# Last two head groups share one score unit: joining two half-filled units and keeping the emptied slot

## The chip, the cores and the metric

The kernel runs on one core of a Trainium2 chip. The metric is the device time of one execution in microseconds. Three runs of the kernel before gave 320.46, 319.23 and 320.46 us; the median is 320.46 us. One further execution was recorded by the hardware profiler, and all intervals below come from it.

## The reference

The input is a sequence of 2048 tokens with 640 features in bfloat16. It passes a layer norm and then two branches, whose product is added to the input:

```
xn = layernorm(x)
s  = attention(xn, wq, wk, wv, wo, beta)      # 32 heads of 20, in 4 segments of 512 tokens
g  = silu( (sigmoid(xn @ w_gate) * (xn @ w_up)) @ w_down )   # 640 -> 1536 -> 640
out = x + s * g
```

In the attention branch every segment of 512 tokens attends causally to itself only (softmax of q k / sqrt(20)). What earlier segments held comes in through a memory matrix per head, which is updated after each segment. A gate per head, sigmoid(beta), mixes the two.

## The kernel before, in words

**Segments and slots.** The four segments are worked through one after the other. The scores of a segment are cut by *head group* (4 heads, one per quarter of TensorE's rows; 8 groups, numbered 0 to 7) and by *key block* (128 keys; 4 blocks per segment, 0 to 3). Because the mask is causal, key block kb is met by the last 512 - 128 kb queries only. One entry `(g, kb, c0, ncol, q0)` says: group g, key block kb, put into columns c0 to c0 + ncol of the score tile, for the queries from q0 on. A *unit* is a list of such entries that together fill up to 512 columns of the score tile `Sps` (128 x 4 x 512 in PSUM, one buffer). A unit costs one *slot*.

**How units are formed.** `pair_units(g)` packs two head groups into five units: block 0 of g; blocks 1 and 3 of g; blocks 2 of g and of g + 1 together (256 + 256 columns); block 0 of g + 1; blocks 1 and 3 of g + 1. The last pair of the last segment, groups 6 and 7, is different: `single_units` gives each of them three units of its own, and block 2 stands alone in a unit of 256 columns. So there are 15 pairs of five units and one of six, 81 slots (numbers 0 to 80). Slots 75, 76, 77 are group 6; slots 78, 79, 80 are group 7; slots 77 and 80 are the half-filled ones.

**What a slot does.** `scores` (L548) writes the unit's scores into `Sps` with matmuls that use a quarter of TensorE's rows each. `exps` makes one ScalarE exponential over the unit (L556) into a tile `pt` (four buffers), and one GpSimd select per entry (L558), which zeroes the keys behind the mask. Then the slot is filled with *dense* work: `do_gate`, `do_up` and `do_down` matmuls (lines 130 and 134), which come from a queue `dense` and are handed out one matmul at a time. At the end of the last segment, these are the `yp` matmuls of `do_down`: 12 of them per tile, then a tanh on ScalarE (`t`, L454) and a multiply on VectorE (`aa`, L455).

**What orders the work.** The program is written out engine by engine. Events carry a time in slots (table `TIMES`), and a running account of matmul time (`due` against `done`, `rate` per slot) decides how many dense matmuls lie between two events. The account spreads all remaining work evenly over `SLOTS` slots.

**How probabilities meet values.** For all groups but 6 and 7 of the last segment, `attend_T` takes a whole group at once. Groups 6 and 7 of the last segment (slots from `OLD` = 75) use `attend` (L612): with time 1.36 slots after a unit's slot began, it multiplies that unit's `pt` with the values into `Aps`, one PSUM tile for the whole group with a place for each of the four query blocks. A matmul there has 21 output columns, and there are 4 heads times (4 - kb) query blocks for an entry. For group 7, `attend` calls `finalize` twice: after its third block of keys for query blocks 0 and 1, after its fourth for 2 and 3. For group 6 it calls it once. `finalize` is four VectorE instructions: reciprocal of the sums (L631), times the gate (L632), times `Aps` (L636, tile `od`), and an addition into `odot` (L638). L631 and L636 read `Aps`.

**The tail.** Two `do_down` items are held back. After the last slot: the first held item, `tail_T4` (two transposes of `odot` into `po`, L523, copied to `oT` on ScalarE, L524), then the `attend` of the last unit (slot 80), then for each of four token tiles two `tail_piece` (five matmuls with the output weights, L532, then a VectorE multiply, L534) and `tail_add` with the store, with the second held item and a second `tail_T4` between them.

Of the kernel before, what the change touches and what calls it, by code (L numbers as in the profile page):

```python
# [14 lines left out]
NSEG = 4  # L15
# [4 lines left out]
NG = 8  # L20
# [23 lines left out]
def pair_units(g):  # L44
    return [[(g, 0, 0, 512, 0)],
            [(g, 1, 0, 384, 128), (g, 3, 384, 128, 384)],
            [(g, 2, 0, 256, 256), (g + 1, 2, 256, 256, 256)],
            [(g + 1, 0, 0, 512, 0)],
            [(g + 1, 1, 0, 384, 128), (g + 1, 3, 384, 128, 384)]]

def single_units(g):
    return [[(g, 0, 0, 512, 0)],
            [(g, 1, 0, 384, 128), (g, 3, 384, 128, 384)],
            [(g, 2, 0, 256, 256)]]

def segment_units(n):
    units = []
    for g in range(0, NG, 2):
        last = n == NSEG - 1 and g == NG - 2
        units += single_units(g) + single_units(g + 1) if last else pair_units(g)  # L60
    return units

TIMES = dict(
# [18 lines left out]
def kernel(  # L82
# [437 lines left out]
    def tail_T4(j0, j1):  # L520
        po = ps_d.tile([P, 2, P], BF, name="po", tag="d")
        for j in range(j0, j1):
            nc.tensor.transpose(po[:, j - j0, :], seg[NSEG - 1]["odot"][:, j, C4:D], ident[:])  # L523
        nc.scalar.copy(seg[NSEG - 1]["oT"][:, DC - 1, j0 * P:j1 * P].rearrange("p (j t) -> p j t", t=P), po[:])  # L524

    def tail_piece(j, half):

        s, hs = seg[NSEG - 1], slice(half * HD, (half + 1) * HD)
        sp = ps_d.tile([P, HD], F32, name="sp", tag="d")
        for c in range(DC):  # L530
            oT = s["oTm" if c == 3 else "oT"]
            nc.tensor.matmul(sp[:], lhsT=oT[:, c, j * P:(j + 1) * P], rhs=Wo[:, c, hs],  # L532
                             start=(c == 0), stop=(c == DC - 1), skip_group_check=True)
        nc.vector.tensor_tensor(s["aa"][j][:, hs], s["aa"][j][:, hs], sp[:], op=ALU.mult)  # L534
# [10 lines left out]
    def scores(unit):  # L545
        for r in range(4):
            for (g, kb, c0, ncol, q0) in unit:
                nc.tensor.matmul(Sps[:, r, c0:c0 + ncol],  # L548
                                 lhsT=KT[32 * r:32 * r + DH + 3, g, kb * P:(kb + 1) * P],
                                 rhs=QT[32 * r:32 * r + DH + 3, g, q0:L],  # L550
                                 start=True, stop=True, tile_position=(32 * r, 0))

    def exps(unit):
        ntot = sum(u[3] for u in unit)
        pt = ptp.tile([P, 4, L], BF, name="pt")
        nc.scalar.activation(pt[:, :, 0:ntot], Sps[:, :, 0:ntot], ACT.Exp, scale=SCALE)  # L556
        for (g, kb, c0, ncol, q0) in unit:
            nc.gpsimd.affine_select(out=pt[:, :, c0:c0 + P], in_=pt[:, :, c0:c0 + P], compare_op=ALU.is_ge,  # L558
                                    fill=0.0, base=0, pattern=[[0, 4], [1, P]], channel_multiplier=-1)
        return pt  # L560

    def attend_T(n, g, todo):


        s = seg[n]
        if g % 4 == 0:
            s["obT", g // 4] = opool.tile([P, 4, L], BF, name="obT", bufs=1)
        ps = ps_d.tile([P, L], F32, name="ApsT", tag="d")
        for i, ((_, kb, c0, ncol, q0), t) in enumerate(todo):
            for r in range(4):  # L570
                off = (kb * H + 4 * g + r) * E1
                nc.tensor.matmul(ps[32 * r:32 * r + 32, q0:L], lhsT=Vflat[n % 2][:, off:off + 32],  # L572
                                 rhs=t[:, r, c0:c0 + ncol], start=(i == 0), stop=(i == len(todo) - 1),
                                 tile_position=(0, 32 * r), skip_group_check=True)
        tb = opool.tile([P, L // 32, 32], F32, name="tb", tag="tb", bufs=1)
        rb = opool.tile([P, L // 32], F32, name="rb", bufs=2)
        ob = obs[g % 2]

        def quotients():
            nc.vector.reciprocal(rb[:], tb[:, :, DH])  # L580
            if g == NG - 1:
                nc.vector.scalar_tensor_tensor(out=ob[:, :, 0:DH], in0=tb[:, :, 0:DH], scalar=omgT[:, g:g + 1],
                                               in1=rb[:].unsqueeze(2).to_broadcast([P, L // 32, DH]),
                                               op0=ALU.mult, op1=ALU.mult)
                return
            nc.gpsimd.tensor_scalar(rb[:], rb[:], omgT[:, g:g + 1], None, op0=ALU.mult)
            nc.gpsimd.tensor_tensor(ob[:, :, 0:DH], tb[:, :, 0:DH],  # L587
                                    rb[:].unsqueeze(2).to_broadcast([P, L // 32, DH]), op=ALU.mult)

        def turn_back():  # L590
            nc.vector.transpose(s["obT", g // 4][:, g % 4, :], ob[:].rearrange("p b e -> p (b e)"))  # L591

        s["turn", g] = (lambda: nc.vector.transpose(tb[:].rearrange("p b e -> p (b e)"), ps[:]),  # L593
                        quotients, turn_back)
# [3 lines left out]
    def attend(n, unit, pt):  # L598

        todo = acc["todo"] + [(p, pt) for p in unit]  # L600
        acc["todo"] = []
        for i, ((g, kb, c0, ncol, q0), t) in enumerate(todo):
            if acc["group"] is None:
                acc["group"], acc["blocks"], acc["fresh"] = g, 0, True
                acc["ps"] = ps_d.tile([P, 4, 4, E1], F32, name="Aps", tag="d")
            if acc["group"] != g or (acc["blocks"] == 0 and i > 0 and todo[i - 1][0][0] != g):
                acc["todo"] = todo[i:]
                break
            for r in range(4):
                for qb in range(kb, 4):  # L610
                    off = c0 + (qb - kb) * P
                    nc.tensor.matmul(acc["ps"][:, qb, r, :], lhsT=t[:, r, off:off + P],  # L612
                                     rhs=V[n % 2][:, kb, 4 * g + r, :],
                                     start=acc["fresh"], stop=True, skip_group_check=True)
                    acc["fresh"] = False
            acc["blocks"] += 1
            split = g == NG - 1
            if acc["blocks"] == 3 and split:
                finalize(n, g, 0, 2)
            if acc["blocks"] == 4:  # L620
                finalize(n, g, 2 if split else 0, 4)
                acc["group"] = None
                acc["todo"] = todo[i + 1:]
                break
# [134 lines left out]
    held = [dense.pop() for _ in range(2)]  # L759

    units = [(n, unit) for n in range(NSEG) for unit in segment_units(n)]
    SLOTS, SEG = len(units), 20
    LAST = (NSEG - 1) * SEG
    OLD = LAST + 15
    events = []
    pts = {}
# [5 lines left out]
    for p in range(0, OLD, 5):  # L772
        n, g = units[p][0], units[p][1][0][0]
# [16 lines left out]
    def old_attend(slot):  # L790
        attend(NSEG - 1, units[slot][1], pts[slot])
# [95 lines left out]
    def complete():  # L887

        while cur[0] is not None:
            step()  # L890
# [8 lines left out]
    def fill(want):  # L899
        while done < want and (cur[0] is not None or dense and may(dense[0][0])):  # L900
            step()

    for slot, (n, unit) in enumerate(units):
        if slot in visits:
            m, g, us = visits[slot]
            attend_T(m, g, [(q, pts[u]) for u in us for q in units[u][1] if q[0] == g])
            done += AV_NS
        scores(unit)
        pts[slot] = exps(unit)
        ORDER["columns"] = slot + 1 in visits  # L910
        due += rate
        own = []
        while events and events[0][0] < slot + 1:
            own.append(events.popleft())
        free = max(0.0, due - done - sum(e[2] for e in own))
        begin = done
        for t, _, ns, fn in own:
            fill(begin + free * (t - slot))
            if ns > 0:
                inside[0] += 1  # L920
                if inside[0] > 2:
                    complete()
            fn()
            done += ns
            begin += ns
        fill(due)
        if cur[0] is not None and cur[0][0] * cur[0][1] < TIMES["rest"]:
            complete()
    fill(1e12)
    finish(held[1][3])  # L930
    tail_T4(0, 2)
    old_attend(SLOTS - 1)
    tail_piece(0, 0)
    tail_piece(0, 1)
    tail_add(0, 0, 2, nc.gpsimd, nc.sync)
# [43 lines left out]
```

## Time and profile before

| What | Value |
|---|---|
| Median of three runs | 320.46 us (319.23 to 320.46) |
| Profiled execution, first to last instruction | 317.6 us, between 1.6 and 2.9 us less than the three runs |
| TensorE busy (matmul) | 309.7 us, 98% |
| VectorE, ScalarE, GpSimd busy | 229.5 (72%), 227.2 (72%), 135.5 us (43%) |
| Exponentials, L556, 81 times | 150.3 us, 1.856 us each |
| Exponential of a half-filled unit | 1.02 us, against 1.88 us for a full one |
| Selects, L558, 128 times | 83.2 us, 0.665 us each |
| Score matmuls, L548 | 32.6 us busy in 512 |
| `attend` matmuls, L612 | 80, all between 290.2 and 306.6 us, 0.172 us each, overlapping |
| Mean granted TensorE clock | 0.999 |

How to read it: the profile names an instruction by engine, line, output and inputs. Start and duration are microseconds from the span's start. Matmuls are pipelined, so the duration of one (0.30 us for a `yp` matmul) is longer than the distance from one to the next; costs on TensorE are therefore read from start to start. PEld is the loading of weights, which runs beside the matmuls. In square brackets stands how long an engine had been idle before an instruction, and what ended that.

### The profile page before, as it was taken

Reading aid. Unit: us, or ns where it says so; the run is one execution under the profiler, and the core shown is the slowest. Engines: PE = TensorE matmul, PEld = TensorE weight load, DVE = VectorE, ACT = ScalarE, POOL = GpSimd, SP = SyncE. Lnnn points to the kernel's source line nnn. Section 1 sums busy time; section 2 is a strip of 40 time slices with the busy share of each in tenths; the row PEclk is TensorE's granted clock in tenths of the full one; section 3 lists DMA queues with packets and bytes.
Section 4 is the critical chain, followed back from the end, with each engine's and each line's share of the span. In section 5 each row is a group of like instructions: output and inputs, shape, how many; then the busy total and the mean of one; then the engine's idle time right before and its main releaser. Section 6 shows DMA issues by size and latency. Waiting matters only on the chain.

```text
span 317.6 us, 10049 instructions
## 1 busy us (share of the span) xinstructions
PE 309.7 (98%) x4215; PEld 167.1 (53%) x4244; DVE 229.5 (72%) x505; ACT 227.2 (72%) x229; POOL 135.5 (43%) x230
## 2 busy tenths in 40 slices
PE   8999999999999999999999999999999999999995
PEld 3544445665555445654665455545466645445673
DVE  6474356755869888997779999977787686734565
ACT  3723477788898877778898868678897766777631
POOL 1870036535263445334453354444533353535322
PEclk9999999999999999999999999999999999999999
DMA  7984886420752462505954443238533000350302
GB/s 252 364 328 142 289 221 191 105 46 2 215 158 62 130 130 85 126 23 173 240 168 122 114 110 109 82 121 210 168 82 120 19 23 23 114 137 4 99 20 83
DMA packets 56085, 41.36 MB, mean 130 GB/s; under 512 B 26952, under 2 KB 54664, under 8 KB 56040
## 3 DMA queue, kind: packets, MB, share of 16 engines
q1 hardware_dynamic: 53496, 35.97, 39.7%
q10 hardware_dynamic: 2544, 4.75, 4.0%
q8 instruction: 33, 0.54, 0.7%
q14 instruction: 12, 0.10, 0.1%
HBM read 19.90 MB, written 14.78 MB: 109 GB/s over the span
## 4 chain that ended last, share of the span: by engine, by line
PE 96%; issue 1%; ACT 1%; DVE 1%; ACTq 0%
PE yp L130 11%; PE up L130 11%; PE gp L130 10%; PE psq L130 10%; PE Sps L548 9%; PE gp L134 6%; PE up L134 6%; PE yp L134 6%; PE psv L130 6%; PE ApsT L572 5%; PE psq L134 4%; PE sp L130 3%; PE sp L134 3%; PE sp L532 2%; PE psv L134 1%; PE wps L644 1%
## 5 line engine op out<-in xcount | busy, mean ns | idle before, releaser
L556 ACT ACTIVATE pt<-Sps 128x2048 bf16<-128x2048 f32 (+1 forms) x81 | 150.3, 1856 | 40.8 <-PE Sps L548 35.9
L558 POOL TENSOR_SCALAR_AFFINE_SELECT pt<-pt 128x512 bf16<-128x512 bf16 x128 | 83.2, 665 | 157.6 <-ACT pt L556 157.5
L438 DVE SCALAR_TENSOR_TENSOR hT<-tg,up 128x512 bf16<-128x512 bf16 x48 | 32.4, 675 | 23.2 <-PE up L130 8.7
L130 PE MATMUL up<-xnT,Wu 128*128 128x512 bf16 x147 | 40.3, 380 | 1.2 <-issue 1.0
L130 PE MATMUL yp<-Wd,hT 128*128 128x320 bf16 x257 | 40.1, 300 | 0.0
L427 ACT ACTIVATE tg<-gp 128x512 bf16<-128x512 f32 x48 | 28.6, 596 | 14.4 <-PE gp L130 11.0
L130 PE MATMUL gp<-xnT,Wg 128*128 128x512 bf16 x144 | 38.1, 379 | 0.3 <-issue 0.2
L548 PE MATMUL Sps<-QT,KT 23*128 23x128 bf16 (+3 forms) x512 | 32.6, 301 | 0.2
L591 DVE STREAM_TRANSPOSE obT<-ob 128x512 bf16<-128x512 bf16 x30 | 21.1, 705 | 13.4 <-POOL ob L587 13.3
L130 PEld LDWEIGHTS <-hT 128*128 128x128 bf16 x257 | 23.5, 98 | 11.6 <-issue 3.0
L455 DVE SCALAR_TENSOR_TENSOR aa<-t,yp 128x320 bf16<-128x320 bf16 x32 | 15.3, 480 | 13.8 <-ACT t L454 13.7
L134 PE MATMUL gp<-xnT,Wg 128*32 128x512 bf16 x360 | 24.1, 380 | 0.0
L548 PEld LDWEIGHTS <-KT 23*128 23x128 bf16 x512 | 10.0, 92 | 24.5 <-issue 24.1
L130 PEld LDWEIGHTS <-Wu 128*128 128x128 bf16 x160 | 14.3, 98 | 16.2 <-issue 3.2
L593 DVE STREAM_TRANSPOSE tb<-ApsT 128x512 f32<-128x512 f32 x30 | 21.2, 708 | 2.2 <-PE ApsT L572 2.1
L572 PE MATMUL ApsT<-pt,V 128*32 128x512 bf16 (+2 forms) x480 | 22.7, 299 | 0.0
L130 PEld LDWEIGHTS <-Wg 128*128 128x128 bf16 x150 | 14.1, 98 | 16.0 <-issue 1.9
L134 PE MATMUL up<-xnT,Wu 128*32 128x512 bf16 x320 | 21.7, 380 | 0.0
L454 ACT ACTIVATE t<-yp 128x320 bf16<-128x320 f32 x32 | 13.9, 435 | 10.2 <-PE yp L130 8.5
L130 PE MATMUL psv<-Wv,xnT 128*128 128x320 bf16 x130 | 20.6, 299 | 0.2
L587 POOL TENSOR_TENSOR ob<-tb,rb 128x320 bf16<-128x320 f32 x27 | 19.8, 733 | 2.3
L134 PE MATMUL yp<-Wd,hT 128*32 128x320 bf16 x508 | 20.0, 300 | 0.0
(122 smaller groups left out, 448.7 us busy)
## 6 DMA issues: line engine op xcount, KB each, us to landing
KT<-Kd SPq DMA_DIRECT2D x32, 80.0 KB
QT<-Qd SPq DMA_DIRECT2D x32, 80.0 KB
out_dram<-xt SPq DMA_DIRECT2D x14, 160.0 KB
Wg<-in_B_w_gate_dram ACTq DMA_DIRECT2D x1, 1920.0 KB
Wu<-in_B_w_up_dram ACTq DMA_DIRECT2D x1, 1920.0 KB
xt<-in_A_x_dram SPq DMA_DIRECT2D x3, 640.0 KB
Wd<-in_B_w_down_dram SPq DMA_DIRECT2D x1, 1920.0 KB
Xd<-xn SPq DMA_DIRECT2D x12, 160.0 KB
```

The source lines that it names most:

```text
L130: nc.tensor.matmul(out_, lhsT=lhsT, rhs=rhs, start=start, stop=stop, skip_group_check=True)
L134: nc.tensor.matmul(out_[cols], lhsT=lhsT[:, cols], rhs=rhs, start=start, stop=stop, tile_position=(0, 32 * r), skip_group_check=True)
L427: nc.scalar.activation(tg[:], gp[:], ACT.Tanh, scale=0.5)
L438: nc.vector.scalar_tensor_tensor(out=h[:], in0=seg[n]["tg"][:], scalar=1.0, in1=up[:], op0=ALU.add, op1=ALU.mult)
L455: nc.vector.scalar_tensor_tensor(out=s["aa"][j][:, hs], in0=t2[:], scalar=1.0, in1=yp[:], op0=ALU.add, op1=ALU.mult)
L548: nc.tensor.matmul(Sps[:, r, c0:c0 + ncol], lhsT=KT[32 * r:32 * r + DH + 3, g, kb * P:(kb + 1) * P], rhs=QT[32 * r:32 * r + DH + 3, g, q0: ...
L556: nc.scalar.activation(pt[:, :, 0:ntot], Sps[:, :, 0:ntot], ACT.Exp, scale=SCALE)
L558: nc.gpsimd.affine_select(out=pt[:, :, c0:c0 + P], in_=pt[:, :, c0:c0 + P], compare_op=ALU.is_ge, fill=0.0, base=0, pattern=[[0, 4], [1, P ...
L572: nc.tensor.matmul(ps[32 * r:32 * r + 32, q0:L], lhsT=Vflat[n % 2][:, off:off + 32], rhs=t[:, r, c0:c0 + ncol], start=(i == 0), stop=(i == ...
L587: nc.gpsimd.tensor_tensor(ob[:, :, 0:DH], tb[:, :, 0:DH], rb[:].unsqueeze(2).to_broadcast([P, L // 32, DH]), op=ALU.mult)
L591: nc.vector.transpose(s["obT", g // 4][:, g % 4, :], ob[:].rearrange("p b e -> p (b e)"))
L593: s["turn", g] = (lambda: nc.vector.transpose(tb[:].rearrange("p b e -> p (b e)"), ps[:]), quotients, turn_back)
```

## The change

All sixteen pairs of head groups now take five units, the last pair included. So slot 77 holds block 2 of group 6 and block 2 of group 7; slots 78 and 79 are group 7 as before; and slot 80 has no unit. It stays in the list as `(NSEG - 1, None)`, so `SLOTS` is still 81 and the account of dense work is unchanged, but `scores` and `exps` are not called in it. The `attend` of slots 75 to 79 stays at its place in the events; block 2 of group 7 is taken up by the `attend` of slot 78, ahead of block 0. The `attend` in the tail goes. Group 7 thus gets its blocks in the order 2, 0, 1, 3 instead of 0, 1, 3, 2, and both of its `finalize` calls fall into the `attend` of slot 79: the first between the matmuls of block 1 and those of block 3.

```diff
-def single_units(g):
-    return [[(g, 0, 0, 512, 0)],
-            [(g, 1, 0, 384, 128), (g, 3, 384, 128, 384)],
-            [(g, 2, 0, 256, 256)]]
-
 def segment_units(n):
     units = []
     for g in range(0, NG, 2):
-        last = n == NSEG - 1 and g == NG - 2
-        units += single_units(g) + single_units(g + 1) if last else pair_units(g)
+        units += pair_units(g)
     return units
...
     units = [(n, unit) for n in range(NSEG) for unit in segment_units(n)]
+    units.append((NSEG - 1, None))
...
-        scores(unit)
-        pts[slot] = exps(unit)
+        if unit is not None:
+            scores(unit)
+            pts[slot] = exps(unit)
...
     tail_T4(0, 2)
-    old_attend(SLOTS - 1)
     tail_piece(0, 0)
```

## The prediction

> **What bounds the kernel now.** I read the page's busy times first, then its chain of work, then the timeline of the last 20 us, where everything in the change lies.
>
> ```profile
> span 317.6 us, 10049 instructions
> ...
> PE 309.7 (98%) x4215; PEld 167.1 (53%) x4244; DVE 229.5 (72%) x505; ACT 227.2 (72%) x229; POOL 135.5 (43%) x230
> ...
> PEclk9999999999999999999999999999999999999999
> ...
> PE 96%; issue 1%; ACT 1%; DVE 1%; ACTq 0%
> ```
>
> TensorE is busy 98% of the span, and 96% of the chain that ended last is TensorE. The list of waits names no TensorE wait for another engine after the first two microseconds; what little there is, is weight loads in the tail. So here the time is the sum of TensorE's steps: a microsecond that is added on TensorE, busy or waiting, is a microsecond of the kernel, and work saved on ScalarE or GpSimd (72% and 43% busy) is worth nothing by itself.
>
> Next the timeline around slot 80, the slot that loses its scores:
>
> ```profile
> 299.78 1.65 PE L130 MATMUL yp<-Wd,hT 128*128 128x320 bf16 x11
> ...
> 301.37 0.29 PE L548 MATMUL Sps<-QT,KT 23*128 23x256 bf16 x4
> ...
> 301.59 1.12 PE L130 MATMUL yp<-Wd,hT 128*128 128x320 bf16 x7
> ...
> 302.55 0.55 PE L612 MATMUL Aps<-V,pt 128*128 128x21 bf16 x16
> ...
> 302.96 3.28 PE L130 MATMUL yp<-Wd,hT 128*128 128x320 bf16 x23
> 303.15 0.49 DVE L455 SCALAR_TENSOR_TENSOR aa<-t,yp 128x320 bf16<-128x320 bf16 x1 [0.76 <-ACT t L454]
> 303.56 0.20 DVE L631 RECIPROCAL rd<-Aps 128x8 f32<-128x8 f32 x1
> 303.79 0.17 DVE L632 TENSOR_TENSOR rd<-rd,omg 128x8 f32<-128x8 f32 x1
> 303.99 0.32 DVE L636 TENSOR_TENSOR od<-Aps,rd 128x160 bf16<-128x160 f32 x1
> ```
>
> A yp matmul follows the one before after (1.65 - 0.30) / 10 = 0.135 us. From this the price of what lies between two runs of yp can be read. The eleven from 299.78 would have gone on at 299.78 + 11 x 0.135 = 301.265, but the next starts at 301.59: the half-filled score block costs 0.325 us. The sixteen attend matmuls cost 302.96 - (301.59 + 7 x 0.135) = 0.425 us. In the same way, from the rows above these: the full block of slot 79 (yp from 296.49 to 298.42) 0.435, the full one of slot 78 (293.41 to 295.32) 0.425, and eight attend matmuls of slot 77 (295.32, seven yp, 296.49) 0.225 us.
>
> **The change part by part.** I also compared the instructions of both programs engine by engine. Dense work keeps its order, and the account of dense matmuls is unchanged, so only what is named here moves.
>
> 1. Slot 77 takes eight score matmuls of 256 columns instead of four. No row shows that shape. Bounds are 0.325 us (the second four hidden) and 0.65 (two half blocks). I take 0.43, the two full blocks, which stream the same 512 columns per row group: +0.105 us.
>
> 2. Slot 77's exponential grows from 1.02 to 1.88 us and gets a second select of 0.64. Before, it started at 292.15; so it ends near 294.1. The next scores come at 294.99, the attend that reads it at 296.28, and GpSimd has finished its `ob` at 294.07. All of it hides behind yp: 0. Without that cover the price would be 0.86 us.
>
> 3. Slot 78's attend has 24 matmuls instead of 16: +0.20 us by the difference of the two rows above.
>
> 4. Slot 80 loses its score block: -0.325 us. Its exponential (1.02) and select (0.64) lay beside yp: 0.
>
> Up to the attend of slot 79, TensorE is therefore shifted by 0.105 + 0.20 - 0.325 = -0.02 us: nothing.
>
> 5. **A new wait.** In the changed program's list, the attend of slot 79 has twelve matmuls for block 1, and then the first matmul of block 3 waits for VectorE; counting the semaphore's steps, it is for L636, the last of the first `finalize` that reads `Aps`. Both use one PSUM tile; that the columns differ does not spare it. Before, the four matmuls of block 3 came ahead of that `finalize`, and nothing touched `Aps` until 306.19. Behind the waiting matmul stand, in order, three attend matmuls and all remaining yp, so TensorE stops.
>
> How long? On VectorE, `finalize` stands behind the `aa` of the yp tile that TensorE finished just before (one yp matmul of the next tile lies between), and that waits for its tanh. Nothing before shows TensorE waiting on this chain, but the chain itself ran in the tail:
>
> ```profile
> 306.08 0.28 PE L523 MATMUL po<-ident,odot 128*128 128x128 bf16 x2
> ...
> 306.19 0.35 PE L612 MATMUL Aps<-V,pt 128*128 128x21 bf16 x8
> 306.28 0.44 ACT L454 ACTIVATE t<-yp 128x320 bf16<-128x320 f32 x1 [1.19 <-PE yp L130]
> ...
> 306.39 0.57 PE L532 MATMUL sp<-Wo,oT 128*128 128x320 bf16 x3
> 306.61 0.37 ACT L524 COPY oT<-po 128x256 bf16<-128x256 bf16 x1
> ...
> 306.75 0.49 DVE L455 SCALAR_TENSOR_TENSOR aa<-t,yp 128x320 bf16<-128x320 bf16 x1 [0.20 <-ACT t L454]
> 306.80 0.30 PE L532 MATMUL sp<-Wo,oTm 128*128 128x320 bf16 x1
> 307.03 0.39 PEld L532 LDWEIGHTS <-oT 128*128 128x128 bf16 x4 [0.27 <-ACT oT L524]
> ...
> 307.15 0.20 DVE L631 RECIPROCAL rd<-Aps 128x8 f32<-128x8 f32 x1
> ...
> 307.59 0.32 DVE L636 TENSOR_TENSOR od<-Aps,rd 128x160 bf16<-128x160 f32 x1
> ```
>
> The last of the 23 yp starts at 302.96 + 3.28 - 0.30 = 305.94. The tanh starts 0.34 later, `aa` 0.47 after it, the reciprocal 0.40 after that, and L636 ends at 307.59 + 0.32 = 307.91: 1.97 us from the last yp start. For the step from a releaser's end to TensorE I take the copy above, 306.61 + 0.37 = 306.98 to 307.03: 0.05 us.
>
> In the changed kernel, the 17th yp after slot 78's attend ends the tile. It starts at 299.78 + 0.105 + 0.20 + 16 x 0.135 = 302.245; so TensorE is released at 302.245 + 1.97 + 0.05 = 304.265. It gets there after one more yp (0.135), the 0.15 from a yp to the first attend matmul (302.55 less 302.40) and 12 x 0.0256 (0.41 / 16): 302.84. The stall is **1.42 us**. Low bound: if the reciprocal were not behind `aa`, it would follow the twelfth matmul's end, about 303.0, and the chain (307.91 - 307.15 = 0.76) gives 303.8, a stall of 1.0. High bound: if the release came with L638 (0.24, 0.04 later), 1.70. I take 1.42, as every link of it is a row.
>
> The same place, seen from the Trainium skill: "PSUM — Partial Sum Buffer", section "PSUM bank collisions raise a hardware error", says to guard PSUM by bank and quadrant, not by address, because two engines in one bank collide even on different columns. By it the wait is needed and the sum is this one; by columns alone, the sum would be that of the first rival. No trace here shows a collision.
>
> The wait for GpSimd's second select (the two end at 302.49 before, about 0.1 later after) lies inside the stall: 0.
>
> 6. The tail loses eight attend matmuls between `po` and the first output product (306.19 to 306.39: 0.20 us of TensorE) and four VectorE instructions. But the fifth product needs the ScalarE copy of `po`, which stands behind the tanh of the last yp tile; before, TensorE already idled for it at 307.03. The copy comes no earlier, so TensorE waits 0.20 longer: 0. The bound is -0.20, if the copy came first. The freed VectorE time (307.15 to 308.18) lets the first `aa` times `sp` go 0.8 us earlier, but the next products are released with 1 us to spare; 0. The end (last matmul 313.93, two VectorE steps, the store) keeps its shape.
>
> **Sum:** -0.02 + 1.42 + 0 = +1.40 us; with the bounds, 0.7 to 1.9. The span goes from 317.6 to 319.0. The three runs lie 1.6 to 2.9 us above the profiled span, the median 2.86, which I keep: 320.46 + 1.40 = **321.86 us**, 0.44% slower.
>
> **Rivals.**
>
> *The wait is not felt (not slower).* If VectorE had read `Aps` before TensorE gets to block 3, only the sums of 1 to 4 and of the tail are left: -0.02, with the tail's bound -0.22, so 320.2 to 320.5, say 320.4. It decides at 302.84: L636 has to end before. For: VectorE is idle between 302.39 and 303.15. Against: the tile's last yp starts only 0.6 us before TensorE gets there, and the chain needs 1.97.
>
> *VectorE is later than that.* Two instructions ahead of `finalize` there is the addition L487, which waits for a load (1.06 us idle, start 300.94, 1.05 long). After it and one `aa`, VectorE is free at 302.39, and needs to be by 303.05. If the load lands over 0.66 us later, the stall grows by the rest; 1.5 us later gives +2.2 and 322.7. The single trace can't tell how far that load varies.
>
> *The clock falls.* In the windows view the granted clock stays at 1.00 until 316.5, is 0.73 from 316.5 to 317 and 0.50 after; the last matmul ended at 313.93. So it took about 2.8 us without matmuls to halve; 1.42 is half of that. If the pause did halve it, 20 yp at double distance would cost 20 x 0.135 = 2.7 us more: 324.6. "TensorE: Matmul & The Clock Gate", section "What's actually happening" (the Trainium skill), puts it at an idle window of about 3.4 us that runs freely; by it the clock stays too.
>
> **Chances.** Forecast 0.80, wait not felt 0.10, VectorE later 0.07, clock 0.03. The range takes in the bounds and the first rival's upper end, with the 0.4% by which the runs differ: 320.4 to 322.9. A measurement of this kernel can tell about 0.5% from no change, 1.6 us here, and 1.40 lies just under it: of the forecast's 0.80, I give 0.30 to more than 1.6 us, because the stall's upper bound and the spread reach past it. Slower by over 0.5%: 0.30 + 0.10 = 0.40; within: 0.50 + 0.07 = 0.57; faster: 0.03, the far end of the first rival.
>
> **What would show it.** In the changed profile: TensorE idle for about 1.4 us inside the L612 group near 302.8, ended by VectorE's `od`, with four matmuls behind it; one score block of about 0.43 in slot 77 and none in slot 80; both `finalize` runs before 305.5; in the tail `po`, then `sp` at once, and the wait for ScalarE's `oT` grown from 0.27 to about 0.45; granted clock 1.00. I am wrong if L612 runs through without a gap, or if the gap lies elsewhere: at slot 77's attend (a late select) or before `po`.

## The result, and the profile after

Over twelve runs each, the changed kernel took 320.89 us (median; 320.64 to 322.43) and the kernel before 319.56 us (319.21 to 321.05). The ratio is 1.0044, with a 95% interval from 1.0029 to 1.0059: 0.44% slower, as forecast. The span of the profiled execution is 319.0 us, against 317.6.

The `single_units` lines that the change removes shift all later lines by six: `attend` is now L606, `finalize` L625 to L632, `scores` L542, `exps` L550 and L552, `do_down` L448 and L449, the tail L517 to L528. First the page of the changed kernel:

```profile
span 319.0 us, 10076 instructions
...
PE 311.4 (98%) x4244; PEld 167.2 (52%) x4244; DVE 229.8 (72%) x505; ACT 227.4 (71%) x228; POOL 135.4 (42%) x230
...
PEclk9999999999999999999999999999999999999999
```

TensorE is busy 98% as before and its clock is unchanged. Its busy time is 1.7 us more. But 4244 matmuls are on record against 4215, while both programs hold the same number: some are missing from the trace of before, and this line can't tell where the time went. The list of TensorE's waits does (columns: engine, tile and line, releaser, that is, what ended the wait; us in total, how often, the longest). This line was not there before:

```profile
engine line waited for: us in total, times, longest us
PE Aps L606 <- DVE od L630: 1.3, 1, 1.3
```

One wait, once, 1.3 us. The timeline shows it in place (start, duration, engine, line, operation; in brackets the idle time before it):

```profile
299.38 0.75 PE L606 MATMUL Aps<-V,pt 128*128 128x21 bf16 x24
...
299.99 2.60 PE L124 MATMUL yp<-Wd,hT 128*128 128x320 bf16 x18
...
302.43 0.45 PE L606 MATMUL Aps<-V,pt 128*128 128x21 bf16 x12
302.49 0.44 ACT L448 ACTIVATE t<-yp 128x320 bf16<-128x320 f32 x1 [1.19 <-PE yp L124]
302.96 0.49 DVE L449 SCALAR_TENSOR_TENSOR aa<-t,yp 128x320 bf16<-128x320 bf16 x1 [0.56 <-ACT t L448]
303.37 0.20 DVE L625 RECIPROCAL rd<-Aps 128x8 f32<-128x8 f32 x1
303.61 0.17 DVE L626 TENSOR_TENSOR rd<-rd,omg 128x8 f32<-128x8 f32 x1
303.81 0.32 DVE L630 TENSOR_TENSOR od<-Aps,rd 128x160 bf16<-128x160 f32 x1
...
304.18 0.25 PE L606 MATMUL Aps<-V,pt 128*128 128x21 bf16 x4 [1.30 <-DVE od L630]
...
304.28 3.28 PE L124 MATMUL yp<-Wd,hT 128*128 128x320 bf16 x23
```

The reader is to follow the numbers down the VectorE rows. TensorE runs the twelve matmuls of block 1 from 302.43; the thirteenth, at 0.0256 us each, was due at 302.74. But tanh, `aa`, reciprocal, gate and `od` (L630) come first, one after the other, and L630 ends at 304.13. TensorE goes on at 304.18, 1.44 us late. The profile says 1.30 because it counts idle time from the modelled end of the last matmul, not from the moment at which the next was due.

The tail:

```profile
307.40 0.28 PE L517 MATMUL po<-ident,odot 128*128 128x128 bf16 x2
...
307.51 0.57 PE L526 MATMUL sp<-Wo,oT 128*128 128x320 bf16 x3
307.60 0.44 ACT L448 ACTIVATE t<-yp 128x320 bf16<-128x320 f32 x1 [1.19 <-PE yp L124]
...
307.94 0.37 ACT L518 COPY oT<-po 128x256 bf16<-128x256 bf16 x1
...
308.35 0.39 PEld L526 LDWEIGHTS <-oT 128*128 128x128 bf16 x4 [0.47 <-ACT oT L518]
308.36 0.72 PE L526 MATMUL sp<-Wo,oT 128*128 128x320 bf16 x4
308.71 0.49 DVE L528 TENSOR_TENSOR aa<-aa,sp 128x320 bf16<-128x320 bf16 x1
```

The products follow the transposes at once, and the wait for the copy `oT` has grown from 0.27 to 0.47 us. From `po` to the fifth product it is 0.96 us, against 0.95 before: the eight attend matmuls that left the tail gave nothing.

Single spans are a poor measure of such a change: profiled executions reached slot 77 anywhere between 291.70 and 293.44 us, with the same instructions up to there. So below I use one **stretch** that is free of that: from the start of slot 77's score block to the start of the last output product. Its two ends in the kernel before:

```profile
291.81 0.29 PE L548 MATMUL Sps<-QT,KT 23*128 23x256 bf16 x4
...
313.63 0.30 PE L532 MATMUL sp<-Wo,oT 128*128 128x320 bf16 x1
```

And in the changed kernel:

```profile
291.70 0.41 PE L542 MATMUL Sps<-QT,KT 23*128 23x256 bf16 x8
...
314.96 0.30 PE L526 MATMUL sp<-Wo,oT 128*128 128x320 bf16 x1
```

It was 313.63 - 291.81 = 21.82 us before and 314.96 - 291.70 = 23.26 after, 1.44 us more.

### The profile page after: what moved, and what is told of

The parts are those of the page before. It is cut to its first block, busy times and chain, and to the rows that moved or that the text cites. A ratio compares the mean times of both kernels' runs of the same rounds, so it can differ in the third digit from the quotient of the medians.

```text
span 319.0 us, 10076 instructions
## 1 busy us (share of the span) xinstructions
PE 311.4 (98%) x4244; PEld 167.2 (52%) x4244; DVE 229.8 (72%) x505; ACT 227.4 (71%) x228; POOL 135.4 (42%) x230
## 4 chain that ended last, share of the span: by engine, by line
PE 95%; DMA 2%; ACT 1%; DVE 1%; issue 0%; SPq 0%; ACTq 0%
PE up L124 11%; PE yp L124 11%; PE gp L124 10%; PE psq L124 10%; PE Sps L542 9%; PE gp L128 6%; PE up L128 6%; PE yp L128 6%; PE psv L124 5%; PE ApsT L566 5%; PE psq L128 4%; PE sp L124 3%; PE sp L128 3%; DMA Wv<-in_A_wv_dram 2%; PE sp L526 1%; PE psv L128 1%
## 5 line engine op out<-in xcount | busy, mean ns | idle before, releaser
L550 ACT ACTIVATE pt<-Sps 128x2048 bf16<-128x2048 f32 x80 | 150.2, 1878 | 40.2 <-PE Sps L542 35.4
L552 POOL TENSOR_SCALAR_AFFINE_SELECT pt<-pt 128x512 bf16<-128x512 bf16 x128 | 83.0, 665 | 156.8 <-ACT pt L550 156.7
L124 PE MATMUL up<-xnT,Wu 128*128 128x512 bf16 x160 | 43.0, 380 | 0.0
L124 PE MATMUL gp<-xnT,Wg 128*128 128x512 bf16 x150 | 39.3, 380 | 0.0
L542 PE MATMUL Sps<-QT,KT 23*128 23x384 bf16 (+3 forms) x512 | 32.4, 300 | 0.2
L449 DVE SCALAR_TENSOR_TENSOR aa<-t,yp 128x320 bf16<-128x320 bf16 x32 | 15.3, 479 | 15.1 <-ACT t L448 14.9
L566 PE MATMUL ApsT<-pt,V 128*32 128x512 bf16 (+2 forms) x480 | 22.8, 299 | 0.0
L448 ACT ACTIVATE t<-yp 128x320 bf16<-128x320 f32 x32 | 14.0, 437 | 12.2 <-PE yp L124 10.3
L542 PEld LDWEIGHTS <-KT 23*128 23x128 bf16 x512 | 9.9, 92 | 24.3 <-issue 23.9
L128 PE MATMUL up<-xnT,Wu 128*32 128x512 bf16 x320 | 21.7, 380 | 0.0
```

Of the source, the lines that this page charges most:

```text
L124: nc.tensor.matmul(out_, lhsT=lhsT, rhs=rhs, start=start, stop=stop, skip_group_check=True)
L128: nc.tensor.matmul(out_[cols], lhsT=lhsT[:, cols], rhs=rhs, start=start, stop=stop, tile_position=(0, 32 * r), skip_group_check=True)
L449: nc.vector.scalar_tensor_tensor(out=s["aa"][j][:, hs], in0=t2[:], scalar=1.0, in1=yp[:], op0=ALU.add, op1=ALU.mult)
L542: nc.tensor.matmul(Sps[:, r, c0:c0 + ncol], lhsT=KT[32 * r:32 * r + DH + 3, g, kb * P:(kb + 1) * P], rhs=QT[32 * r:32 * r + DH + 3, g, q0: ...
```

## The experiments

The theory: the 1.4 us are TensorE standing in front of block 3's first matmul until `finalize` has read `Aps`. The rival: the joining itself costs it, through the fuller unit of slot 77, its longer exponential and second select, and the 24 matmuls of slot 78. All ratios are to the kernel before.

| Run | Stretch, us | Expected, us | Median, us | Ratio (95% interval) |
|---|---|---|---|---|
| before | 21.82 | | 319.56 | |
| changed | 23.26 | 23.22 | 320.89 | 1.0044 (1.0029 to 1.0059) |
| both `finalize` last | 21.81 | 21.8 | 319.68 | 1.0001 (0.9991 to 1.0011) |
| wait alone, in the kernel before | 23.34 | 23.3 | 321.62 | 1.0054 (1.0041 to 1.0067) |
| attend later | 22.82 | 22.8 | 320.71 | 1.0033 (1.0020 to 1.0046) |
| two PSUM tiles | 21.97 | 21.8 to 22.0 | 320.01 | 1.0005 (0.9995 to 1.0014) |
| block 3 in the tail | 21.72 | 21.7 | 319.52 | 0.9989 (0.9977 to 1.0001) |
| transposes early | 21.40 | 21.4 to 21.5 | 319.48 | 0.9980 (0.9962 to 0.9997) |
| before, transposes early | 21.71 | 21.7 | 319.55 | 0.9986 (0.9976 to 0.9996) |
| loaded piece last | 21.77 | 21.35 to 21.45 | 319.74 | 0.9991 (0.9977 to 1.0006) |

The rows from the third to the sixth are compared with one set of runs of the kernel before (median 319.64), the last four with another (319.98). "Wait alone" and "attend later" ran five times each, "both `finalize` last" and "two PSUM tiles" eleven times, the others twelve.

The expectations of the third to the sixth row were put as spans, and three of these four spans came out longer than expected: 318.0 us against 317.4 to 317.7 (both `finalize` last), 319.6 against 318.5 (attend later), 318.5 against 317.6 to 317.8 (two tiles); the wait alone gave 319.2 against 319.1. The three had reached slot 77 later than the kernel before by 0.35, 0.98 and 0.68 us, ahead of all that their edits touch. For these rows the table therefore gives as expected the 21.82 us of before plus the expected change of the span; the last four rows were expected as stretches.

**Both finalize calls last.** The change stays, the wait goes:

```diff
-            if acc["blocks"] == 3 and split:
-                finalize(n, g, 0, 2)
             if acc["blocks"] == 4:
+                if split:
+                    finalize(n, g, 0, 2)
```

> The changed kernel, but both finalize calls of group 7 come after the four matmuls of block 3, so nothing on TensorE waits for them. Theory (the wait of block 3 for L636 of the kernel before is the whole cost, 1.42 us): the gap in the attend of slot 79 is gone, span 317.6 us as before (-0.2 to +0.1), 1.4 us under the changed kernel, ratio to before 1.000. Rival (the joining itself costs it: the full unit of slot 77, its longer exponential and two selects, the 24 matmuls in slot 78): as the changed kernel, ratio 1.004.

The same place in its timeline:

```profile
302.89 0.55 PE L606 MATMUL Aps<-V,pt 128*128 128x21 bf16 x16
...
303.29 3.28 PE L124 MATMUL yp<-Wd,hT 128*128 128x320 bf16 x23
```

Sixteen matmuls in one piece, and the next yp 0.40 us after their start. The whole loss is gone, with the fuller unit, the two selects and the 24 matmuls all in place. The rival falls.

**The wait alone, in the kernel before.** The converse: no joining, only the wait.

```diff
-            if acc["blocks"] == 3 and split:
+            if acc["blocks"] == 2 and split:
```

> The kernel before with all its units, but the first finalize of group 7 is called after its second key block (blocks 0 and 1 are all that query blocks 0 and 1 need), so that the matmuls of block 3 wait for it. Theory: TensorE comes to block 3 at 302.86 and is released by L636, which ended at 304.31 before: a gap of about 1.5 us, span 319.1, ratio 1.0047. Rival (the joining costs it): as before, ratio 1.000.

```profile
302.57 0.45 PE L612 MATMUL Aps<-V,pt 128*128 128x21 bf16 x12
...
304.01 0.32 DVE L636 TENSOR_TENSOR od<-Aps,rd 128x160 bf16<-128x160 f32 x1
...
304.39 0.25 PE L612 MATMUL Aps<-V,pt 128*128 128x21 bf16 x4 [1.37 <-DVE od L636]
```

The thirteenth matmul was due at 302.57 + 12 x 0.0256 = 302.88 and started at 304.39: 1.51 us. It is a little longer than in the changed kernel, because here slot 80 still has its exponential, and the tanh ahead of `aa` stands behind it on ScalarE. So the wait is enough to make the loss, and taking it out is enough to lose it.

**The attend later.** Is the gap a fixed latency, or the rest of a chain that started earlier?

```diff
-        at(slot + 1 + TIMES["attend"], 500, old_attend, slot)
+        at(slot + 1 + TIMES["attend"] + 0.25 * (slot == SLOTS - 2), 500, old_attend, slot)
```

> The changed kernel with the attend of slot 79 a quarter of a slot later; four more yp matmuls stand ahead of it. Theory: the aa that stood ahead of the reciprocal is then nearly through (it ends at 303.45 in the changed kernel), so the reciprocal starts when the twelfth matmul is done, about 303.45; 0.76 us later L636 ends and TensorE, which came at 303.28, goes on at 304.25. The gap shrinks by the four yp (0.54 us) to about 0.95 us, span 318.5, ratio 1.0028. If the gap were only a fixed latency between the engines, it would stay 1.4 us and the ratio 1.0044.

```profile
304.06 0.49 DVE L449 SCALAR_TENSOR_TENSOR aa<-t,yp 128x320 bf16<-128x320 bf16 x1 [0.56 <-ACT t L448]
304.07 0.45 PE L606 MATMUL Aps<-V,pt 128*128 128x21 bf16 x12
304.55 0.21 DVE L625 RECIPROCAL rd<-Aps 128x8 f32<-128x8 f32 x1
...
305.00 0.32 DVE L630 TENSOR_TENSOR od<-Aps,rd 128x160 bf16<-128x160 f32 x1
...
305.37 0.25 PE L606 MATMUL Aps<-V,pt 128*128 128x21 bf16 x4 [0.86 <-DVE od L630]
```

Four more yp stand before the attend (22 instead of 18). TensorE was due at 304.38 and went on at 305.37: 0.99 us. So the gap is no fixed latency. About a third of the 1.44 us was the `aa` queued ahead of `finalize`. The rest is `finalize` itself: its reciprocal starts at 304.55, when the twelfth matmul is done (304.07 + 0.45 = 304.52), and no longer 0.41 us after the start of `aa`, as in the changed kernel.

**Two PSUM tiles.** Query blocks 0 and 1 accumulate in one tile, 2 and 3 in another; `finalize` stays between blocks 1 and 3.

```diff
-                acc["group"], acc["blocks"], acc["fresh"] = g, 0, True
-                acc["ps"] = ps_d.tile([P, 4, 4, E1], F32, name="Aps", tag="d")
+                acc["group"], acc["blocks"] = g, 0
+                acc["ps"] = [ps_d.tile([P, 4, 4, E1], F32, name="Aps", tag="d")] * 2
+                if g == NG - 1:
+                    acc["ps"][1] = ps_d.tile([P, 4, 4, E1], F32, name="Bps", tag="d")
+                acc["fresh"] = [True, True]
...
+                    half = qb // 2 if g == NG - 1 else 0
-                    nc.tensor.matmul(acc["ps"][:, qb, r, :], lhsT=t[:, r, off:off + P],
+                    nc.tensor.matmul(acc["ps"][half][:, qb, r, :], lhsT=t[:, r, off:off + P],
...
-                                     start=acc["fresh"], stop=True, skip_group_check=True)
-                    acc["fresh"] = False
+                                     start=acc["fresh"][half], stop=True, skip_group_check=True)
+                    acc["fresh"][half] = False
...
-        s, Aps = seg[n], acc["ps"]
+        s, Aps = seg[n], acc["ps"][q0 // 2]
```

> The changed kernel, but group 7 accumulates query blocks 0 and 1 in one PSUM tile and 2 and 3 in another; finalize stays between blocks 1 and 3. Theory (the wait is there because both halves share one tile): no gap in the attend. The second tile takes a buffer from yp, whose next tile waits for the aa that ends at 302.40 when TensorE comes at about 302.28: up to 0.15 us. Span 317.6 to 317.8, ratio 1.000 to 1.001. Rival (order of the calls, or the joining): 319.0, ratio 1.004.

```profile
300.77 2.76 PE L124 MATMUL yp<-Wd,hT 128*128 128x320 bf16 x18
...
302.71 0.47 DVE L449 SCALAR_TENSOR_TENSOR aa<-t,yp 128x320 bf16<-128x320 bf16 x1
...
303.38 0.17 PE L610 MATMUL Aps<-V,pt 128*128 128x21 bf16 x1
...
303.63 0.30 PE L610 MATMUL Bps<-V,pt 128*128 128x21 bf16 x6
...
303.78 3.28 PE L124 MATMUL yp<-Wd,hT 128*128 128x320 bf16 x23
```

The attend is L610 here, and the second tile is `Bps`. There is no gap in the attend: it starts at 303.38 and yp follows at 303.78. The order of calls is that of the changed kernel, so it is the shared tile that makes the wait. This fits the section of "PSUM — Partial Sum Buffer" (the Trainium skill) that the prediction names, if the two buffers lie in different banks, which no trace here shows; what an unguarded read beside a write to one bank would do was not run. The price is there too: 18 yp take 2.61 us from their start to the attend instead of 2.44, because the next yp tile has to wait for a buffer until `aa` ends at 303.18. It shows as 0.15 us in the stretch.

**Block 3 in the tail.** The wait stays in the program, but 23 yp lie ahead of it.

```diff
     def old_attend(slot):
-        attend(NSEG - 1, units[slot][1], pts[slot])
+        last = slot == SLOTS - 2
+        attend(NSEG - 1, units[slot][1][:1] if last else units[slot][1], pts[slot])
...
     tail_T4(0, 2)
+    attend(NSEG - 1, units[SLOTS - 2][1][1:], pts[SLOTS - 2])
     tail_piece(0, 0)
```

> The changed kernel, but only block 1 of group 7 is multiplied at its place in slot 80; block 3's four matmuls and the second finalize go to the tail, where the attend of slot 80 stood before, so the first finalize still comes between them. Theory (a wait costs only what the waiting engine stands idle; 23 yp, 3.1 us, now lie between): no gap in the attend, and the four matmuls (0.10 us) fall into the time in which TensorE waits for the copy of po. From slot 77's score block to the last product 21.7 us, against 21.82 before and 23.26 in the changed kernel; ratio 0.9996. Rival (the order finalize, then block 3, in itself): 23.2 us, ratio 1.004.

```profile
303.51 0.45 PE L606 MATMUL Aps<-V,pt 128*128 128x21 bf16 x12
...
303.82 3.28 PE L124 MATMUL yp<-Wd,hT 128*128 128x320 bf16 x23
...
306.94 0.28 PE L517 MATMUL po<-ident,odot 128*128 128x128 bf16 x2
...
307.05 0.25 PE L606 MATMUL Aps<-V,pt 128*128 128x21 bf16 x4
```

The same dependence costs nothing 3 us later, and the four matmuls vanish in the wait for the copy.

**Transposes early.** On top of the run with both `finalize` last, the tail's transposes move ahead of work that hides their copies. This needs the joining: only then is group 7 finished before the tail.

```diff
-    finish(held[1][3])
+    for _ in range(4):
+        next(held[1][3])
     tail_T4(0, 2)
+    finish(held[1][3])
...
+    tail_T4(2, 4)
     finish(held[0][3])
...
     tail_add(1, 0, 1, nc.vector)
-    tail_T4(2, 4)
```

> Both finalize calls after block 3 (as in the run with both last), and in the tail each pair of transposes moved ahead: the first after four of the twelve yp of the first held item, the second ahead of the second held item, which is possible only because group 7 is finished before the tail. Theory (the tail's eight attend matmuls were given back by the wait for the copy of po, 0.33 us, and 0.08 at the second copy): these waits go, from slot 77's score block to the last product 21.4 to 21.5 us; the product that takes the late load of oTm may still wait 0.07. Ratio 0.9987. If the copies were not what TensorE waited for: 21.8 us, 1.000.

```profile
306.60 0.28 PE L517 MATMUL po<-ident,odot 128*128 128x128 bf16 x2
...
306.72 1.25 PE L124 MATMUL yp<-Wd,hT 128*128 128x320 bf16 x8
...
307.59 0.42 DVE L512 TENSOR_TENSOR oTm<-oTm,oT 96x512 bf16<-96x512 bf16 x1
...
307.80 0.57 PE L526 MATMUL sp<-Wo,oT 128*128 128x320 bf16 x3
...
308.21 0.30 PE L526 MATMUL sp<-Wo,oTm 128*128 128x320 bf16 x1
...
308.35 0.71 PE L526 MATMUL sp<-Wo,oT 128*128 128x320 bf16 x4
```

The five products run through at 0.135 us. The stretch is 0.42 us shorter than before, and the ratio lies below 1 by its interval: by both, this version beats both kernels, if only just. By time alone the lead over the kernel before is not firm. That kernel gave 319.56, 319.64 and 319.98 us in three sets of runs, and against the first two the 319.48 us of this version would be only 0.08 and 0.16 us less.

**The kernel before with its first transposes early.** What is the joining worth in that?

```diff
-    finish(held[1][3])
+    for _ in range(4):
+        next(held[1][3])
     tail_T4(0, 2)
+    finish(held[1][3])
```

> The kernel before, with only its first pair of transposes moved ahead by eight yp; the second cannot move, since group 7 is finished only in the tail. Theory: the idle 0.10 us ahead of the fifth product goes, the eight attend matmuls stay: 21.7 us from slot 77's score block to the last product, against 21.82 before; ratio 0.9997. So the joining is worth the other 0.3 us of the run with both transposes early. If the joining were worth nothing there: 21.4 to 21.5 us.

```profile
307.52 0.30 PE L532 MATMUL sp<-Wo,oTm 128*128 128x320 bf16 x1
...
307.66 0.71 PE L532 MATMUL sp<-Wo,oT 128*128 128x320 bf16 x4
```

The fifth product follows the fourth after 0.14 us instead of 0.23 (306.80 to 307.03 before). The stretch is 21.71 us: 0.11 of the 0.42 us come without the joining, 0.31 with it. The times of the two runs (319.55 and 319.48 us) cannot tell them apart, so this division rests on the traces alone. The ratio of 0.9986 would be 0.45 us, more than the stretch shows; where that comes from stays open. The 319.98 us to which it refers is itself 0.34 us above the other set of the kernel before.

**The loaded piece last.** On top of the run with transposes early, the product that uses `oTm`, the tile that a transfer brings, comes last of the five.

```diff
-        for c in range(DC):
+        for i, c in enumerate((0, 1, 2, 4, 3)):
...
-                             start=(c == 0), stop=(c == DC - 1), skip_group_check=True)
+                             start=(i == 0), stop=(i == DC - 1), skip_group_check=True)
```

> As the run with both transposes early, and the product that needs the late load (oTm) comes last of the five instead of fourth. Theory: the last 0.07 us of waiting for that load goes; 21.35 to 21.45 us from slot 77's score block to the last product, ratio 0.9985. If nothing waited for the load there, as the run with both transposes early.

This missed. The timeline, with the load (SPq), VectorE's addition to what it brought (L512) and the products:

```profile
302.24 1.16 SPq L508 DMA_TRANSPOSE oTm<-Od  x1
...
306.62 0.71 PE L526 MATMUL sp<-Wo,oT 128*128 128x320 bf16 x4
...
307.05 0.42 DVE L512 TENSOR_TENSOR oTm<-oTm,oT 96x512 bf16<-96x512 bf16 x1 [0.73 <-DMA oTm<-Od]
...
307.53 0.31 PE L526 MATMUL sp<-Wo,oTm 128*128 128x320 bf16 x1 [0.20 <-DVE oTm L512]
```

The product with `oTm` was due at 306.62 + 4 x 0.135 = 307.16 and came at 307.53. The load landed late in this execution: L512 starts 4.81 us after the issue, against 4.43 before and 4.25 in the run with transposes early. Without that 0.37 us the stretch would be 21.40, the same as in that run. There the five products had already run through without a wait, so there was nothing left to gain: the 0.07 us that the expectation counted on had not occurred. So putting the piece last did no harm that shows, but it doesn't cover what this load can vary, and in this execution, with the copies out of the way, the load was the next bound of the tail.

## Why the prediction was right, point by point

**Slot 77's scores (+0.105).** From the block's start to the next yp it is 0.34 us (291.70 to 292.04), 0.22 before (291.81 to 292.03): +0.12. One of the two blocks from which the price was taken is a little off: by the prediction's own 0.135 us for each yp, slot 79's comes to 298.42 - 296.49 - 11 x 0.135 = 0.445 us, not 0.435. The term would move by 0.01 at most.

**Longer exponential and second select (0).** The exponential runs from 292.17 to 294.05, the two selects end at 295.35, and the attend that needs them starts at 296.29 as before.

**Slot 78's attend (+0.20).** From its start to the next yp 0.61 us (299.38 to 299.99), 0.40 before: +0.21.

**Slot 80's scores (-0.325).** Up to the attend of slot 79 the changed kernel lies 0.12 us ahead (302.43 against 302.55), and 0.11 of that it already had at slot 77: a net shift of -0.01, forecast -0.02.

**The wait (1.42).** 1.44 measured. Its links: last yp of the tile at 299.99 + 16 x 0.135 = 302.15, tanh 0.34 later, `aa` 0.47, reciprocal 0.41, end of L630 0.76, together 1.98 (forecast 1.97); release 0.05 as taken from ScalarE. That the chain was copied from another place where it had run, queue and all, made it exact. The low bound of 1.0 us, `finalize` without the `aa` ahead, is what the later attend showed (0.99).

**The tail (0).** As forecast: the copy stands behind the tanh, and the 0.20 us went into the wait for it. The freed VectorE time moved the first `aa` times `sp` 0.7 us nearer to `po` (1.31 instead of 2.02), where 0.8 was forecast, and gained TensorE nothing: from the fifth product to the last it took 6.60 us in both kernels.

**The rivals.** "The wait is not felt" is out by the 1.44 us gap. "VectorE is later" did not occur: the `aa` before it ended at 302.40, 0.56 us ahead of need. A single trace could not tell how far the load ahead of L487 varies, but ten can: the addition starts between 2.80 and 3.01 us after the second of the two transfers `oT<-OTd` was issued (L483; L477 and L481 in the changed kernels), a spread of 0.21 us where this rival needs more than 0.66. "The clock falls" did not occur either. In the windows view of the changed kernel (after the busy times of the five engines come the granted clock, the DMA share and GB/s):

```profile
302.70:304.20 1.50, 0.20 (x9) 0.12 (x6) 1.13 (x5) 0.23 (x1) 0.00 (x0) 1.00 0.39 87
```

The clock stays at 1.00 in the gap, and in the windows after it. That agrees with what "TensorE: Matmul & The Clock Gate" (the Trainium skill, "What's actually happening") says of a window of about 3.4 us; a gap near that length was not run.

**The absolute time.** 321.86 us was forecast and 320.89 measured. The difference is in the base: the median of 320.46 rested on three runs, and twelve give 319.56. The step that gave it way was to add 2.86 us to a span of 317.6, which joins two different executions: in every run whose span is on record the device time lies 1.66 to 1.79 us above that run's own span. With 1.7 the forecast span of 319.0 would have given 320.7. The step itself was 1.33 us by medians and 1.44 by the stretch, against 1.40. The sum was right, and its split as well; only the level to which it was added was 0.9 us high. That the absolute time still fell into the range of 320.4 to 322.9 was in part luck. The bounds of the step, 0.7 to 1.9 us, on 320.46 give 321.16 to 322.36, and 320.89 lies below them. With the stated 0.4% on either side they would have given about 319.9 to 323.6, so the stated ends are not that sum either. It was the reach down to the first rival's 320.4 that took the measured time in, and that rival's mechanism was wrong.

## What to carry to other kernels

When pieces of work are reordered, look for the reads that were placed to come after the last write of a tile: here a reader that slipped between two groups of writes to one PSUM tile made TensorE wait 1.44 us, for the reader and for what was queued ahead of it, even though it read other columns than those still to be written. Moving the reader behind the last write, or the last write behind enough other work, cost nothing that the stretch shows; a second tile worked as well, at 0.15 us for the buffer that the pool then lacked. And work taken out of the tail was worth nothing while something else, here a copy behind a tanh, released the next step at the same time.

## What the runs showed of the hardware

The time at which a profiled execution reached slot 77 differed by up to 1.7 us among kernels with equal instructions up to there. Up to 0.5 us of it is there at slot 0 (35.56 to 36.06 us), and the run with transposes early lost 1.6 us on the kernel before between 156 and 178 us. The cause was not followed. Where the addition L512 (L518 before) had to wait for its load, it started 4.25 to 4.81 us after the load's issue. In the kernel before with its first transposes early it started 3.82 us after the issue, so the load can also land sooner.
